# A state-space scan and an MLP on one core: units of one chunk of all four sequences instead of two chunks of one sequence, B and C transposed by VectorE

## The chip, the cores and the metric

One core of one Trainium2 chip. The time is the device time of one execution in microseconds (us), the median of the runs. Five engines work side by side, each through its own queue in order: TensorE (PE in the profile, its weight loads PEld), VectorE (DVE), ScalarE (ACT), GpSimd (POOL), and SyncE (SP), which only issues DMAs here. The tensors lie in the chip's main memory; what the engines read lies in SBUF (128 partitions); PE writes to PSUM (banks of 512 f32 per partition).

## What is computed

Four sequences of 768 steps, 8 heads, head size D = 32, state size N = 16. A scan with decay, chunk by chunk, and then an MLP over all 3,072 tokens (256 to 2,048 to 256, tanh-GELU):

```python
for c in range(nc):
    cum = np.cumsum(la, axis=-1)                        # la = log(clip(a, 1e-6, 1))
    L = np.exp(cum[:, :, :, None] - cum[:, :, None, :]) * causal
    M = np.einsum('bhin,bhjn->bhij', Cc, Bc) * L
    y_intra = np.einsum('bhij,bhjd->bhid', M, xc)
    y_inter = np.einsum('bhin,bhnd->bhid', Cc, state) * decay_to_i[:, :, :, None]
    y[:, :, sl] = y_intra + y_inter
    Bx = np.einsum('bhjn,bhjd->bhjnd', Bc, xc) * decay_from_j[:, :, :, None, None]
    state = decay_full[:, :, None, None] * state + np.sum(Bx, axis=2)
h = x @ w_in                                            # x: y as 3072 tokens x 256
g = 0.5 * h * (1.0 + np.tanh(c * (h + 0.044715 * h * h * h)))
out = g @ w_out
```

The kernels use chunks of 128 steps (the result doesn't depend on the chunk). The decay is put into B and C beforehand: with r the product of a from a step to the end of its chunk, B is multiplied by r and C by 1/r, so the causal product of the two needs only a 0/1 triangle.

## The kernel before

There are 24 chunks of 128 tokens, numbered sequence by sequence. A unit is one or two neighbouring chunks of one sequence (`UNITS`: chunk 0, chunk 1, then pairs; 13 units).

*Preparation per sequence.* `f_R` scans a on DVE into r, for all sequences at once; `f_RT` turns r with matmuls against an identity; `f_recip` takes 1/r. Then per sequence: `f_mul` multiplies B and C (DVE, 128x768), `f_T` turns them by six PE transposes each into PSUM, `f_E` copies them to SBUF (`bh`, `ch`), `f_F` makes `ce` (C with the odd and with the even heads set to zero, `par`), `f_N` turns B back by six more PE transposes and `f_bn` copies that out (`bn`). For the first sequence this is split (`sequence0`), and its first chunk has a short path of its own.

*State part per unit.* `f_G` makes the scores of two heads at a time in one of four row groups of PE (K = 32; partitions 32g to 32g+31 hold two heads), into four banks of PSUM, the tile `gb`. `f_M` multiplies a chunk's scores by the triangle (DVE, 128x1024, PSUM to bf16). `f_D` makes B times x, `f_S` adds it to the decayed state, `f_SP` spreads the state to a block-diagonal `sp_new` (both DVE). `f_Y` adds state and score terms in PSUM (`yb`), in four column groups of 32, and `f_yev` (ACT) evicts it as `xm`, the MLP's input. From unit 4 on, `f_YDG` issues Y of a unit with D and G of the next as one piece.

*MLP per unit.* `f_s1`: up-projection into one of two PSUM tiles `hp` (512 wide: four f-blocks of 128 tokens, or two of 256); `f_gelu` (ACT, 128x512); `f_s2`: down-projection of one chunk, 16 matmuls of 256 into `o_ps`; `f_oev` evicts, `f_store` stores 128 KB.

*Order.* All these are nodes with an engine, an assumed duration, dependencies and a priority. `run_order` plays them through before the kernel is built and fixes every engine's queue; PSUM tiles with one buffer (`gram` is `gb`, `yb`, `o`) are modelled as pools. On the chip each engine works its queue in that order and waits where data is missing. While the plan has PE idle and no down-projection has begun, `idle` puts filler matmuls on zeros (`wz`) in. SP's queue holds all loads but two, and the stores, in the plan's order; a DMA there waits for the one eight before it.

Of the kernel before, what the change touches and what calls it, by code (L numbers as in the profile page):

```python
# [8 lines left out]
FP32 = mybir.dt.float32  # L9
# [84 lines left out]
def kernel(  # L94
# [9 lines left out]
):  # L104
    nc = tc.nc

    batch, H, S, D = x.shape
    N = B.shape[-1]
    Q = 128
    CPB = S // Q  # L110
    R6 = CPB
    NCH = batch * CPB
    HC = CPB // 2
    HS = S // 2
    d_ff = moe_w_in.shape[1]
    d_model = moe_w_in.shape[0]
    n_tokens = batch * S
    NF = d_ff // 128
    UNITS = [[0], [1]] + [[c, c + 1] for c in range(2, NCH, 2)]
    NU = len(UNITS)  # L120

    const = ctx.enter_context(tc.tile_pool(name="const", bufs=1))
    ld = ctx.enter_context(tc.tile_pool(name="ld", bufs=batch))
    wfp = ctx.enter_context(tc.tile_pool(name="wfp", bufs=6))
    ldx = ctx.enter_context(tc.tile_pool(name="ldx", bufs=NU))
    xpool = ctx.enter_context(tc.tile_pool(name="xpool", bufs=6))
    work = ctx.enter_context(tc.tile_pool(name="work", bufs=2))
    msb = ctx.enter_context(tc.tile_pool(name="msb", bufs=4))
    st = ctx.enter_context(tc.tile_pool(name="st", bufs=4))
    GT_BUFS = 6  # L130
    gpool = ctx.enter_context(tc.tile_pool(name="gpool", bufs=GT_BUFS))
    opool = ctx.enter_context(tc.tile_pool(name="opool", bufs=6))
# [5 lines left out]


    a_t = const.tile([64, HS], FP32, name="a_t")  # L140
    a_half = [bass.AP(tensor=a.tensor, offset=a.offset + i * HS, ap=[[S, batch * H], [1, HS]])
              for i in range(2)]
    XF, X16 = {}, {}
    U = [dict() for _ in range(batch)]
    bc0 = const.tile([128, 2, H, N], FP32, name="bc0")

    def load_bc0(i, q):
        q.dma_start(out=bc0[:, i], in_=(B, C)[i][0, :, 0:Q, :].rearrange("h p n -> p h n"))

    def load_bc(b, i):  # L150
        d = U[b]
        if "bc" not in d:
            d["bc"] = ld.tile([128, 2, H, R6 * N], FP32, name="bc_t")
        nc.sync.dma_start(out=d["bc"][:, i],  # L154
                          in_=(B, C)[i][b].rearrange("h (p r) n -> p h (r n)", r=R6))

    nc.sync.dma_start(out=a_t[0:32], in_=a_half[0])
    nc.scalar.dma_start(out=a_t[32:64], in_=a_half[1])
    load_bc0(1, nc.sync)
    load_bc0(0, nc.scalar)  # L160

    wz = const.tile([128, 512], BF16, name="wz")
# [4 lines left out]
    ends = const.tile([64, Q], FP32, name="ends")  # L167
    nc.vector.memset(ends, 0.0)
    nc.vector.memset(ends[:, Q - 1:Q], 1.0)
    ac = const.tile([64, HS + 1], FP32, name="ac")  # L170
    nc.vector.memset(ac[:, HS:HS + 1], 0.0)
    pe1 = const.tile([64, HC], FP32, name="pe1")
    pe2 = const.tile([64, 2 * batch, HC], FP32, name="pe2")

    idf = const.tile([64, 64], FP32, name="idf")
    nc.gpsimd.memset(idf, 0.0)
    nc.gpsimd.affine_select(out=idf, in_=idf, pattern=[[-1, 64]], compare_op=ALU.not_equal,
                            fill=1.0, base=0, channel_multiplier=1)
    ident = const.tile([128, 128], BF16, name="ident")
    make_identity(nc, ident)  # L180
    bmask = const.tile([128, H * D], BF16, name="bmask")
    nc.gpsimd.memset(bmask, 1.0)
    bm3 = bmask.rearrange("p (h d) -> p h d", h=H)
    nc.gpsimd.affine_select(out=bm3, in_=bm3, pattern=[[-N, H], [0, D]],
                            compare_op=ALU.is_ge, fill=0.0, base=0, channel_multiplier=1)
    nc.gpsimd.affine_select(out=bm3, in_=bm3, pattern=[[N, H], [0, D]],
                            compare_op=ALU.is_ge, fill=0.0, base=N - 1, channel_multiplier=-1)
    tri = const.tile([128, Q], BF16, name="tri")
    make_upper_triangular(nc, tri, val=1.0, diag=True)
    tri_b = tri.rearrange("p (o q t) -> p o q t", o=1, q=1).to_broadcast([128, 4, 2, Q])  # L190

    sel8 = const.tile([64, H], FP32, name="sel8")
    nc.vector.tensor_reduce(out=sel8, in_=idf.rearrange("p (b h) -> p h b", h=H),
                            op=ALU.add, axis=mybir.AxisListType.X)
    selp = const.tile([64, H, N], FP32, name="selp")
    nc.vector.tensor_copy(out=selp, in_=sel8.rearrange("p (h o) -> p h o", o=1)
                          .to_broadcast([64, H, N]))
    m8 = const.tile([64, 2 * batch], FP32, name="m8")
    nc.gpsimd.memset(m8, 1.0)
    nc.gpsimd.affine_select(out=m8, in_=m8, pattern=[[-H, 2 * batch]], compare_op=ALU.is_ge,  # L200
                            fill=0.0, base=0, channel_multiplier=1)
    nc.gpsimd.affine_select(out=m8, in_=m8, pattern=[[H, 2 * batch]], compare_op=ALU.is_ge,
                            fill=0.0, base=H - 1, channel_multiplier=-1)
    par = const.tile([128, 2], FP32, name="par")
    bmp = bmask.rearrange("p (g e d) -> p e g d", g=4, e=2)
    for e in range(2):
        nc.vector.tensor_reduce(out=par[:, e:e + 1],
                                in_=bmp[:, e, :, 0:1].rearrange("p g o -> p (g o)"),
                                op=ALU.add, axis=mybir.AxisListType.X)
    r_t = const.tile([64, HS], FP32, name="r_t")  # L210

    rt = const.tile([128, R6, batch * H], FP32, name="rt")
    pt = const.tile([128, R6, batch * H], FP32, name="pt")
    q0 = const.tile([128, H], FP32, name="q0")
    bc0s = const.tile([128, 2, H, N], BF16, name="bc0s")
    ce0 = const.tile([128, 2, Q], BF16, name="ce0")
    bh0 = const.tile([128, Q], BF16, name="bh0")
    pend = const.tile([128, NCH], FP32, name="pend")
    WF = {}
    w_in_sb = const.tile([128, 2, d_ff], BF16, name="w_in_sb")  # L220
    w_out_sb = const.tile([128, NF, d_model], BF16, name="w_out_sb")
    xm = const.tile([128, 2, n_tokens], BF16, name="xm")


    gb = ps1.tile([128, 4, 512], FP32, name="gb")
    yb = ps1.tile([128, 512], FP32, name="yb")
    y4 = yb.rearrange("p (c w t) -> p c w t", c=2, w=2)
    rp0 = yb[:, 0:H]
    T6 = [gb[:, 2 * i, 0:S // 2].bitcast(BF16) for i in range(2)]
    T6_0 = [yb[:, 0:S // 2].bitcast(BF16), T6[1]]  # L230

    T0, DT, MT, RP = {}, {}, {}, {}
    state = {}
    gts, ops, hps, outs = {}, {}, {}, {}

    def load_x(u):
        b, c = divmod(UNITS[u][0], CPB)
        XF[u] = ldx.tile([128, 2, H, D], FP32, name="x_t")
        for k in range(len(UNITS[u])):
            nc.sync.dma_start(out=XF[u][:, k], in_=x[b, :, (c + k) * Q:(c + k + 1) * Q, :]  # L240
                              .rearrange("h p d -> p h d"))

    wi = moe_w_in.rearrange("(k d) f -> d k f", d=128)
    wo = moe_w_out.rearrange("(q p k) m -> q p k m", p=128, k=4)

    def load_wi(q):
        WF[("i", q)] = wfp.tile([128, 2, 512], FP32, name="wf")
        nc.sync.dma_start(out=WF[("i", q)], in_=wi[:, :, q * 512:(q + 1) * 512])  # L248

    def load_wo(q):  # L250
        WF[("o", q)] = wfp.tile([128, 4, d_model], FP32, name="wf")
        nc.sync.dma_start(out=WF[("o", q)], in_=wo[q])  # L252
# [9 lines left out]
    def f_wi(q, k0, k1, eng):  # L262
        for k in range(k0, k1):
            copy(eng, w_in_sb[:, k, q * 512:(q + 1) * 512].rearrange("d (k p) -> d k p", k=4),
                 WF[("i", q)][:, k].rearrange("d (p k) -> d k p", k=4))

    def f_wo(q, eng):
        copy(eng, w_out_sb[:, 4 * q:4 * q + 4], WF[("o", q)])


    def f_clip(i0, i1):
        nc.vector.tensor_scalar(out=ac[:, i0:i1], in0=a_t[:, i0:i1], scalar1=1e-6, scalar2=1.0,
                                op0=ALU.max, op1=ALU.min)

    def f_R(k):
        nc.vector.tensor_tensor_scan(out=r_t[:, k * Q:(k + 1) * Q][:, ::-1],
                                     data0=ac[:, k * Q + 1:(k + 1) * Q + 1][:, ::-1],
                                     data1=ends[:, ::-1], initial=1.0,
                                     op0=ALU.mult, op1=ALU.max)

    def f_RT0():
        nc.tensor.matmul(out=rp0, lhsT=r_t[0:32, 0:Q], rhs=idf[0:32, 0:H], start=True, stop=True,
                         skip_group_check=True)

    def f_RT(r0, r1):
        if r0 == 0:
            RP[1] = psh.tile([128, 512], FP32, name="hp")[:, 0:R6 * batch * H] \
                .rearrange("p (r j) -> p r j", r=R6)
# [524 lines left out]
```

## Time and profile before

| | |
|---|---|
| median of 3 runs | 124.88 us (124.67 to 126.23) |
| span of the profiled execution | 122.8 us |
| up-projection, 256 wide (L506) | 352 matmuls, and 64 of 128 wide |
| down-projection (L523) | 384 matmuls of 128x256 |
| gelu (L514, ACT) | 96 of 596 ns |
| first up-projection | starts at 11.95 us |
| first down-projection | starts at 22.2 us |
| last matmul | ends at 119.02 us |
| x loads | 24 of 128 KB, median 4.5 us from issue to landing (3.3 to 9.1) |
| B and C loads | 8 of 384 KB (4.4 and 5.4 us), 2 of 64 KB (2.8 and 4.2 us) |
| a | 2 of 48 KB (2.0 and 2.3 us) |

The span is that of one execution under the profiler, from its first to its last instruction; 2.1 us lie between it and the median. A group's line reads: line, engine, operation, output from input with shapes, count, then busy us and mean ns of one, then the idle time before them and what ended it. Matmuls overlap, so the pieces of the chain of waits, not the means of a group, tell what one costs in a row.

### The profile page before, as it was taken

The numbers are of one execution on the slowest core, as the hardware profiler recorded it, in microseconds if no ns is written. First come the engines' busy times: TensorE is split into PE (matmuls) and PEld (weight loads), VectorE is DVE, ScalarE is ACT, GpSimd is POOL, SyncE is SP. The second block draws the span as 40 slices with busy tenths as digits, with TensorE's granted clock in tenths as the row PEclk, the third lists the DMA queues.
The fourth block names the chain that finished last, engine by engine and source line by source line (L and its number), as shares of the span: only waits on it lengthen the run. The fifth ranks groups of instructions, "written<-read, shape, count | busy, mean of one in ns | idle before, by whom it ended". The sixth has DMA issues, their size and how long they took to land.

```text
span 122.8 us, 3507 instructions
## 1 busy us (share of the span) xinstructions
PE 114.6 (93%) x1506; PEld 96.2 (78%) x1506; DVE 68.3 (56%) x116; ACT 74.9 (61%) x145; POOL 23.0 (19%) x38
## 2 busy tenths in 40 slices
PE   5899978989799999999999999999999999999970
PEld 5687747778678798787879889787878888888860
DVE  3897999968849888184979672475663000000110
ACT  4025536674676677656686777865768766786310
POOL 7206967750320160122000000000000000000000
PEclk9975699999999999999999999999999999999999
DMA  3999959989799899851101101101110111100121
GB/s 52 242 266 265 328 112 370 320 191 200 128 229 221 127 235 216 145 134 48 43 0 48 43 0 48 43 0 48 43 43 5 45 43 45 45 21 22 43 90 43
DMA packets 40591, 14.09 MB, mean 115 GB/s; under 512 B 35904, under 2 KB 39040, under 8 KB 40576
## 3 DMA queue, kind: packets, MB, share of 16 engines
q1 hardware_dynamic: 39488, 13.75, 46.4%
q8 instruction: 12, 0.20, 0.7%
q10 hardware_dynamic: 1088, 0.11, 0.7%
q14 instruction: 3, 0.02, 0.1%
HBM read 10.72 MB, written 3.15 MB: 113 GB/s over the span
## 4 chain that ended last, share of the span: by engine, by line
PE 70%; SPq 18%; DMA 5%; DVE 3%; issue 1%; DVEq 0%
PE o_ps L523 29%; PE hp L506 29%; SPq L240 7%; DMA bc_t<-in_B_dram 5%; SPq L252 5%; SPq L154 4%; PE yb L523 3%; SPq L248 3%; PE gb L408 2%; PE yb L451 2%; PE yb L460 2%; PE gb L358 2%; DVE ch L260 2%; PE gb L379 1%; DVE bc L349 1%
## 5 line engine op out<-in xcount | busy, mean ns | idle before, releaser
L514 ACT ACTIVATE gT<-hp 128x512 bf16<-128x512 f32 x96 | 53.6, 596 | 24.4 <-PE hp L506 24.2
L506 PE MATMUL hp<-xm,w_in_sb 128*128 128x256 bf16 (+1 forms) x416 | 53.7, 267 | 0.9 <-POOL w_in_sb L258 0.4
L523 PE MATMUL o_ps<-w_out_sb,gT 128*128 128x256 bf16 x352 | 47.3, 273 | 0.0
L506 PEld LDWEIGHTS <-w_in_sb 128*128 128x128 bf16 x416 | 37.6, 99 | 7.7 <-issue 2.0
L523 PEld LDWEIGHTS <-gT 128*128 128x128 bf16 x384 | 37.1, 98 | 4.8 <-issue 0.4
L418 DVE TENSOR_TENSOR m<-gb,tri 128x1024 bf16<-128x1024 f32 (+1 forms) x25 | 29.1, 1173 | 1.9 <-PE gb L408 1.8
L532 DVE COPY o_sb<-o_ps 128x256 f32<-128x256 f32 x2 | 0.8, 424 | 25.6 <-PE o_ps L523 25.6
L258 POOL CAST x<-x_t 128x512 bf16<-128x512 f32 (+1 forms) x12 | 8.5, 710 | 25.0 <-DMA x_t<-in_x_dram 20.1
L479 DVE SCALAR_TENSOR_TENSOR s_new<-s_new,pend,hp 128x64 f32<-128x64 f32 x16 | 4.5, 279 | 11.5 <-PE hp L429 11.2
L776 PE MATMUL o_ps<-wz 128*128 128x128 bf16 x77 | 8.9, 267 | 1.3 <-DVE warm L165 1.3
L530 ACT ACTIVATE o_sb<-o_ps 128x256 f32<-128x256 f32 x20 | 7.7, 385 | 3.8 <-PE o_ps L523 2.1
L486 DVE SCALAR_TENSOR_TENSOR sp_new<-s_new,pend,bmask 128x256 bf16<-128x256 f32 x20 | 10.0, 506 | 0.0
L469 ACT ACTIVATE xm<-yb 128x512 bf16<-128x512 f32 (+1 forms) x13 | 7.3, 564 | 4.3 <-PE yb L460 2.1
L258 POOL CAST w_in_sb<-wf 128x512 bf16<-128x512 f32 x6 | 7.0, 1193 | 7.0 <-DMA wf<-in_moe_w_in_dram 7.0
L776 PEld LDWEIGHTS <-wz 128*128 128x128 bf16 x77 | 6.5, 122 | 1.8 <-DVE warm L165 1.2
L460 PE MATMUL yb<-m,x 128*32 128x128 bf16 x192 | 6.3, 223 | 0.6 <-DVE m L418 0.6
L373 DVE TENSOR_SCALAR ce<-ch,par 128x768 bf16<-128x768 bf16 (+2 forms) x10 | 5.9, 634 | 0.8 <-ACT ch L256 0.8
L451 PE MATMUL yb<-ce,sp_new 128*32 128x128 bf16 x160 | 5.3, 221 | 0.0
L408 PE MATMUL gb<-ce,bh 32*128 32x256 bf16 x96 | 5.1, 278 | 0.0
L460 PEld LDWEIGHTS <-x 128*32 128x32 bf16 x192 | 3.8, 97 | 1.5 <-issue 1.5
L358 PEld LDWEIGHTS <-bc 128*128 128x128 bf16 x48 | 3.8, 110 | 1.3 <-issue 1.1
L258 POOL CAST w_out_sb<-wf 128x1024 bf16<-128x1024 f32 x4 | 4.4, 1112 | 1.5 <-DMA wf<-in_moe_w_out_dram 1.5
(72 smaller groups left out, 61.6 us busy)
## 6 DMA issues: line engine op xcount, KB each, us to landing
x_t<-in_x_dram SPq DMA_DIRECT2D x24, 128.0 KB, 4.5
out_dram<-o_sb SPq DMA_DIRECT2D x24, 128.0 KB, 1.7
wf<-in_moe_w_in_dram SPq DMA_DIRECT2D x4, 512.0 KB, 6.9
wf<-in_moe_w_out_dram SPq DMA_DIRECT2D x4, 512.0 KB, 6.0
bc_t<-in_C_dram SPq DMA_DIRECT2D x4, 384.0 KB, 4.4
bc_t<-in_B_dram SPq DMA_DIRECT2D x4, 384.0 KB, 5.4
bc<-in_B_dram ACTq DMA_DIRECT2D x1, 64.0 KB, 4.2
bc<-in_C_dram SPq DMA_DIRECT2D x1, 64.0 KB, 2.8
```

Of the source, the lines that this page charges most:

```text
L240: nc.sync.dma_start(out=XF[u][:, k], in_=x[b, :, (c + k) * Q:(c + k + 1) * Q, :] .rearrange("h p d -> p h d"))
L258: nc.gpsimd.tensor_copy(out=o, in_=i)
L408: nc.tensor.matmul(out=gb[:, g, 256 * k:256 * k + 256], lhsT=bh_of(gc)[32 * g:32 * g + 32], rhs=ce_of(gc)[32 * g:32 * g + 32], start=True, ...
L418: nc.vector.tensor_tensor(out=MT[gc][:, g0:g1], in0=gb[:, g0:g1, 256 * k:256 * k + 256] .rearrange("p g (e t) -> p g e t", e=2), in1=tri_b ...
L451: nc.tensor.matmul(out=y4[32 * j:32 * j + 32, k, w], lhsT=sp[:, 32 * h:32 * h + 32], rhs=ce_of(gc)[:, h % 2], start=first(j), stop=False, ...
L460: nc.tensor.matmul(out=y4[32 * j:32 * j + 32, k, w], lhsT=X16[u][:, k, 32 * h:32 * h + 32], rhs=m[:, h // 2, h % 2, :], start=first(j), st ...
L486: nc.vector.scalar_tensor_tensor(out=sp_new.rearrange("p (g d) -> p g d", g=4), in0=state[("s", gc)].rearrange("p (o d) -> p o d", o=1).to ...
L506: nc.tensor.matmul(out=hp[:, j * nt:(j + 1) * nt], lhsT=w_in_sb[:, kc, fi * 128:(fi + 1) * 128], rhs=xm[:, kc, t0:t0 + nt], start=(kc == 0 ...
L514: nc.scalar.activation(gts[u][:, i * per:(i + 1) * per, 0:nt], hps.pop((u, i)).rearrange("p (j t) -> p j t", j=per), AF.Gelu_apprx_tanh)
L523: nc.tensor.matmul(out=ops[gc], lhsT=gts[u][:, fi, tt * Q:(tt + 1) * Q], rhs=w_out_sb[:, fi, :], start=(fi == 0), stop=(fi == NF - 1), ski ...
L530: nc.scalar.activation(o_sb, ops.pop(gc), AF.Copy)
L776: nc.tensor.matmul(out=zb[:, 0:128], lhsT=wz[:, 0:128], rhs=wz[:, 0:128], start=True, stop=True)
```

## The change

The whole body is rewritten around another unit: chunk c (0 to 5) of all four sequences, 512 tokens. Partitions 32b to 32b+31 now hold sequence b, with four steps in a partition's row, so a 32x32 block transposes in place on DVE, and row group b of PE works on sequence b.

- B and C come in 32-partition loads of 64 KB, one per chunk, sequence and tensor (48 instead of 10). `f_mul` and the transpose `f_T` are 128x512 per chunk, both DVE. The transposes of r are DVE's too; the reciprocal is one 128x128.
- `bn`, B with steps on partitions, is no longer a transpose: `f_bn` copies `bc16` from SBUF to SBUF, four DMAs of 32 KB per chunk, issued by SP after B's multiply.
- `f_S` keeps the state already decayed, 128x256; its spread form `spb` is written by POOL (`f_sp`, four copies of 32 partitions).
- Y, D and G are separate pieces; G and Y of a chunk come in two halves (w = 0, 1), each with two M.
- The up-projection of chunks 1 to 5 is 512 wide. Chunk 0 goes sequence by sequence, 128 wide.
- w_in is cast without a permutation; its columns are picked with a step of four when loaded as weights.
- The last down-projection, eviction and store are cut in two halves of 128 columns.
- Fillers, durations and priorities are set anew.

```diff
-    UNITS = [[0], [1]] + [[c, c + 1] for c in range(2, NCH, 2)]
+    NC = S // Q
+    R = 4
+    def load_bc(c, i, b, q):
+        t = get("bc", c, [128, 2, H, R * N], FP32)
+        q.dma_start(out=t[32 * b:32 * b + 32, i],
+                    in_=(B, C)[i][b, :, c * Q:(c + 1) * Q, :].rearrange("h (p r) n -> p h (r n)", r=R))
...
-    def f_T(b, i):
-        bc = U[b]["bc16"].rearrange("p i r h n -> p i r (h n)")
-        for r in range(R6):
-            nc.tensor.transpose(out=(T6 if b else T6_0)[i][:, r * 128:(r + 1) * 128], in_=bc[:, i, r], identity=ident)
+    def f_T(c, i):
+        nm = ("bT", "cT")[i]
+        t = get(nm, c, [128, G, Q], BF16)
+        nc.vector.transpose(out=t.rearrange("p g (q r) -> p g r q", r=R),
+                            in_=T[("bc16", c)][:, i].rearrange("p r (g k) -> p g r k", g=G))
...
+    def f_rT(i):
+        nc.vector.transpose(out=rT[i], in_=rr[i].rearrange("q (p r) -> q r p", r=R))
+    def f_qT(i):
+        nc.vector.reciprocal(qT[i], rT[i])
+    def f_bn(c, b):
+        t = get("bn", c, [128, NB, H * N], BF16)
+        nc.sync.dma_start(out=t[:, b], in_=T[("bc16", c)][32 * b:32 * b + 32, 0])
...
+    def f_G(c, w):
+        for g in (2 * w, 2 * w + 1):
+            for b in range(NB):
+                nc.tensor.matmul(out=gb[:, b, 256 * (g % 2):256 * (g % 2) + 256],
+                                 lhsT=T[("bT", c)][32 * b:32 * b + 32, g],
+                                 rhs=T[("ce", c)][32 * b:32 * b + 32, :, g, :],
+                                 start=True, stop=True, tile_position=(32 * b, 0))
+    def f_S(c):
+        d = T[("dt", c)][:, 0:H * D]
+        if c > 0:
+            s = P["st"].tile([128, H * D], FP32, name="st")
+            nc.vector.tensor_tensor(out=s, in0=T[("s", c)], in1=d, op=ALU.add)
+            d = s
+        t = P["st"].tile([128, H * D], FP32, name="st")
+        nc.vector.tensor_tensor(
+            out=t.rearrange("p (g k) -> p g k", g=G), in0=d.rearrange("p (g k) -> p g k", g=G),
+            in1=pend[:, c + 1].rearrange("p (g o) -> p g o", o=1).to_broadcast([128, G, 2 * D]),
+            op=ALU.mult)
+        T[("s", c + 1)] = t
+    def f_sp(c, b, eng):
+        ps = slice(32 * b, 32 * b + 32)
+        copy(eng, spb[c % 2][ps, b], T[("s", c)][ps])
+    def f_s1(c, f):
+        hp = psh.tile([128, 512], FP32, name="hp")
+        T[("hp", (c, f))] = hp
+        for kc in range(2):
+            nc.tensor.matmul(out=hp, lhsT=w_in5[:, kc, f // 4, f % 4], rhs=T[("xm", c)][:, kc],
+                             start=(kc == 0), stop=(kc == 1))
...
+        qn[i] = add("DVE", 0.22, f_qT, i, deps=[rn[i]], prio=p0 + 3)
...
-            def f_YDG(u):
-                f_Y(u)
-                f_D(u + 1)
-                f_G(u + 1)
-            Yn[u] = add("PE", 1.05, f_YDG, u, deps=deps, prio=q + 2)
+            for w in range(2):
+                g = Gn[(c, w)] = add("PE", 0.34, f_G, c, w, deps=[Tn[(c, 0)]] + Fn[c], prio=q + 2 + w)
+                ms = [add("DVE", 1.24, f_M, c, w, kk, deps=[g], prio=q + 2 + w + 0.1 * kk) for kk in range(2)]
+                Mn[(c, w)] = ms
+                g.takes("gA", ms[0]).takes("gB", ms[1])
+                y = Yn[(c, w)] = add("PE", 0.55, f_Y, c, w, deps=ms + xcn[c] + spn[c], prio=q + 4 + w)
```

## The prediction

> **What bounds the kernel now.** I read the page's busy shares and slices first, then the chain of waits, then the groups by shape, then the timeline of the first 40 us.
>
> ```profile
> PE 114.6 (93%) x1506; PEld 96.2 (78%) x1506; DVE 68.3 (56%) x116; ACT 74.9 (61%) x145; POOL 23.0 (19%) x38
> ...
> PEclk9975699999999999999999999999999999999999
> DMA  3999959989799899851101101101110111100121
> ```
>
> TensorE (PE) is full from the eleventh slice on, and nothing else is near full there. DMA is full from the second slice to the sixteenth (3 to 50 us). So there are two stages: one that waits for loads, one that is PE work end to end. The chain says where they meet:
>
> ```profile
> 24.08 5.77 DMA bc_t<-in_B_dram
> ...
> 29.87 0.96 DVE bc L349
> 30.82 0.88 DVE ch L260
> 31.74 0.49 PE gb L358 x6
> ...
> 35.19 0.44 PE o_ps L523 x4
> 35.63 0.33 PE gb L408 x8
> 35.96 0.54 PE o_ps L523 x4
> ...
> 94.32 0.23 PE yb L451 x8
> 94.55 0.11 PE yb L460 x8
> 94.66 0.11 PE yb L451 x8
> 94.77 0.11 PE yb L460 x8
> 94.88 0.98 PE hp L506 x8
> ...
> 119.10 0.42 DVE o_sb L532
> ```
>
> The columns are start, length, what. B of the second sequence lands at 29.9, and from 32 us the chain is PE pieces but for one wait of 0.97 us at 46. The MLP pieces cost 0.109 us per 128x256 matmul (0.87 for 8). An excursion into the state part costs more than itself: the first 8 matmuls of a Y take 0.23 against 0.11 for the next, and 8 MLP matmuls after it 0.98 against 0.87. So a Y with both neighbours is 0.23+0.33+0.11 = 0.67; a G alone 0.33+0.10 = 0.43 (the 4 matmuls behind it take 0.54, not 0.44); a D alone 0.17+0.10 = 0.27. Merged Y, D and G, as at 40.27, make 0.95.
>
> ```profile
> L418 DVE TENSOR_TENSOR m<-gb,tri 128x1024 bf16<-128x1024 f32 x23 | 27.8, 1217 | 1.9 <-PE gb L408 1.8
> L373 DVE TENSOR_SCALAR ce<-ch,par 128x768 bf16<-128x768 bf16 x6 | 2.6, 475 | 0.0
> L373 DVE TENSOR_SCALAR ce<-ch,par 128x384 bf16<-128x384 bf16 x2 | 2.2, 1144 | 0.0
> L305 DVE RECIPROCAL pt<-rt 128x144 f32<-128x144 f32 x1 | 1.0, 1039 | 0.0
> ```
>
> Busy us, then mean ns. The two 384-wide rows are the longer ones: they ran at 12.5 to 14.7 us, under POOL's weight casts (12.44 to 14.6).
>
> **What does not change.** The MLP: 768 matmuls' worth at 0.109 = 83.8 us; up-projections of chunks 1 to 5 become 512 wide, 160 instead of 320. 512-wide is not in the trace: between 0.213 (four times the 0.053 that a 128-wide one adds) and 0.218; I take 0.218, and 0.8 us is the most it can gain. Gelu, M, Y, G and D instructions keep number and shape.
>
> **The late stage, after minus before.** In before, 35.19 to 119.02 (83.8 us) holds the last 656 MLP matmuls of the 256 size (652 recorded) and the state part: pieces of 2.97 G, 4.70 Y, 2.18 transposes, 0.56 D, 0.97 wait, and 1.1 hidden in the neighbours' longer pieces: 12.5 in all. In the changed program's order, chunk 1's first up-projection (call its time T1) also has exactly 656 left: 16 of chunk 0's down-projection and five chunks of 128. Behind it stand eight G, eight Y, three D: 8 x 0.43 + 8 x 0.67 + 3 x 0.33 (sixteen matmuls each, 0.23+0.10) = 9.8, less 0.5 for five places where two of them are neighbours. So PE ends at T1 + 71.5 + 9.3 = T1 + 80.8. The removed PE transposes are worth 2.2 here, their wait 1.0; the unmerged excursions give a part back.
>
> **T1.** It stands behind Y of chunk 1, which wants x of chunk 1 from all four sequences. Time of the 16 DMA engines up to then, by the trace's packets (128 B 13.9 ns, 384 B 25.0, so 256 B some 19.4): an x load 64 packets per engine, 0.89 us; a B or C load now 16 packets, 0.31; weights 1.68 (w_in) and 1.41 (w_out) each. Changed order up to x of chunk 1: a 0.24, B and C of chunk 0 2.5, x 3.5, w_in 6.7, w_out 5.6, B and C of chunk 1 2.5, x 3.5, and eight new SBUF-to-SBUF loads for bn at 0.11 to 0.20: 25.8. The same sum of before up to B of sequence 1 is also 25.8, and that landed at 29.87. So x of chunk 1 lands near 30, 0.5 later if SP's queue starves a little, since the first bn copy waits on SP for DVE's second multiply and everything behind it (w_in 2 and 3, x, w_out) waits too. DVE gets there at: a landed 3.0, clip 0.2, scan 0.4, its transpose 0.25, reciprocal of 128x128 0.94 (1039 ns at 144 and 457 at 48), multiply 0.69, transpose 0.64, multiply 0.69: 7.3, since C's last load lands near 5.2. Some 5 us of loads are then in flight, so the cover is about there. DVE's 128x512 transpose is in no row: 0.32 (ce rate) to 3.1 (reciprocal rate); I take 0.64, the rate of the 128x768 PSUM copy (955 ns). At 3.1 the chain would grow by 2.5 per transpose and the cover be gone.
>
> Then POOL casts the last x (0.61): Y at 31.2. B and C of chunk 1 land at 21.6; multiplies, transposes and ce take 3.4 on DVE, G at 25, two M pairs 2.7 each: 30.5, in time. In PE's queue follow Y 0.67, D 0.33, pp 0.5, 4 MLP 0.44, Y 0.67, 12 MLP 1.31: T1 = 35.1.
>
> **Sum.** PE ends at 35.1 + 80.8 = 115.9. I add 0.5 for G of chunk 2, whose B transpose comes off DVE at 36.0 by the same rows, 0.4 after PE asks. Behind it 3.5 instead of 3.8 (122.8 - 119.02): the last eviction is half a tile, 0.28 (the 128x128 ACT row) for 0.42, and its store half as large. Span 119.9 against 122.8; the median of the runs is 2.1 over that span, so **122.0 us**. What is hidden and priced at nothing: POOL's four 32-partition state copies a chunk (0.11 to 0.43 each; Y is 4 us away; uncovered, 1.7 per chunk), ACT's ce and casts in the first 11 us (PE waits for loads), and the first chunk's x of sequence 2, landing at 16.4 by the same sums: ACT's eleven gelus behind it (0.6) end at 25, while G is awaited anyway.
>
> **Rivals.** *(E) Loads come earlier*: nothing starves, 512-wide is cheaper, no wait at chunk 2: T1 34.3 and 1 us off the rest, 120.1. For it: before's DMA has a dip to 0.31 at 16 to 18 us which the new order need not have.
>
> *(B) DVE held by POOL in chunk 1*: the multiplies and ce fall under w_out casts (1.04 to 1.33 each); with 0.7 for each of four, as the 1144 row has it, M ends at 33.5 and T1 is 36.5. PE would also idle 3 us, with no filler matmuls behind the first down-projection; before, an underfilled stretch was followed by half clock from 7.9 to 14.7. One 3.4 us stretch at half costs 1.7: 123.4 to 125.1, say 124.3.
>
> *(D) Small loads pay latency.* Eight DMAs are in flight at most in either order of waits on SP, and B and C now come as 64 KB. The 64 KB loads of before took 2.8 and 4.2 us to land; eight per 2.8 to 4.2 instead of 2.5, twice before T1, is 0.6 to 3.4 later: 124. The Trainium skill's page "DMA: Bandwidth & Descriptors", section "Rules for kernel authors", speaks against the change here: coalesce small transfers, since under 64 KB mostly overhead is paid. By that rule (D) would be the likeliest and the sum 124; by the rows the packets of a following DMA fill the engines meanwhile (DMA share 0.9 and over with 128 KB x loads).
>
> *(C) The ends swap: slower.* Both queues are fixed. G of each half chunk needs the M pair of the half before it, on the single score tile; M stands in DVE's queue behind the next chunk's multiplies, which wait for loads, and behind a reciprocal which the planner prices at 0.22 against 0.94. PE waits in order, with MLP matmuls queued behind. DVE has 9.1 us of work per chunk (4 M 4.9, two multiplies 1.4, two transposes 1.3, ce 0.7, state 0.8) against 16 of PE, which speaks against it; the 1.8 us for which M waited on G in the row above shows that the hand-over binds when it is late. There are eight such places after T1. Without the 0.5 counted above the sum is 121.5; at 0.42 us of PE wait each the gain is gone, over 0.74 it is slower by more than 2%, and at 1.0 it is 129.5.
>
> *(X) It does not do what it says*: the order shows no PE transpose left, so I give this nothing.
>
> **Chances and range.** Forecast 0.40, E 0.12, B 0.15, D 0.06, C 0.27. Within 2% means 122.4 to 127.4, about what a measurement of this kernel tells from no change. The forecast's own range is 120.8 to 123.4, three fifths of it under 122.4: 0.25 faster, 0.15 same. Faster 0.37, same 0.15 + 0.15 + 0.06 = 0.36, slower 0.27. The range runs from 119.6 (E) to 128.5, into C.
>
> **What would show it.** No PE rows with an identity; 160 512-wide matmuls at some 0.22; last x of chunk 1 cast at 30.6 to 31.5; first 512-wide matmul at 35.1; from there no PE wait over 0.5. Wrong would be: T1 over 37 (B, D), or waits of PE on M or ce of a microsecond in chunk after chunk (C).

## The result and the profile after

The changed kernel takes 142.15 us (median of 4 runs, 141.41 to 142.56), the kernel before 125.48 beside it (4 runs). The ratio is 1.133, 95% interval 1.124 to 1.142: slower. Where a kernel was timed several times, runs more than 1.5% above its fastest are slow ones and stay out of a comparison; here there are none. The profiled execution took 142.56, with a span of 140.9. The page of the changed kernel, busy time and slices:

```profile
PE 118.1 (84%) x1319; PEld 84.7 (60%) x1332; DVE 65.5 (47%) x91; ACT 72.3 (51%) x142; POOL 30.2 (21%) x66
...
PEclk9985557999996899999959999999999999999999
DMA  3897888936478458686484110101111111111121
```

DVE has less work than before (65.5 for 68.3), and DMA, full from 3 to 50 us before, is at 0.3 to 0.8 from the ninth slice to the twenty-second. PE is busy for 84% of the span instead of 93%, and its granted clock dips three times, not once. What PE waited for (in all, times, longest):

```profile
PE hp L402 <- DMA bn<-bc: 5.4, 5, 1.8
PE gb L363 <- DVE bT L310: 5.0, 4, 2.4
PE gb L332 <- DVE bT L310: 3.8, 1, 3.8
```

L402 is D, L363 is G of chunks 1 to 5, L332 the very first G. Between the first 512-wide matmul (T1) and the last matmul, PE's windows show busy time, matmuls recorded and granted clock:

```profile
40.04:137.54 97.50, 84.96 (x869) 0.96 0.33 74
```

T1 came at 40.04, predicted 35.1: 4.9 late. Then 97.5 us follow where 81.3 were predicted (80.8 + 0.5): 16.2 more. Of the 97.5, PE was idle 12.5, and two stretches of 3.4 us ran at half clock, which costs 3.4; the rest is 81.6, so the work itself was sized right to 0.8. Behind the last matmul 3.4 (3.5 predicted), outside the span 1.7 (2.1).

**Ahead of T1.** DVE's timeline of the changed kernel (start, length, what, and in brackets the idle time before it with what ended it):

```profile
19.86 0.29 DVE L280 TENSOR_SCALAR pe<-mR,ac,rr 128x16 f32<-128x16 f32 x1
24.52 0.42 DVE L416 TENSOR_TENSOR st<-hp,pend 128x256 f32<-128x256 f32 x1 [4.38 <-PE yb L350]
24.87 0.68 DVE L302 TENSOR_TENSOR bc<-bc,qT 128x512 bf16<-128x512 f32 x1
25.58 1.36 DVE L310 STREAM_TRANSPOSE cT<-bc 128x512 bf16<-128x512 bf16 x1
26.73 0.72 DVE L302 TENSOR_TENSOR bc<-bc,rT 128x512 bf16<-128x512 f32 x1
27.37 1.59 DVE L319 TENSOR_SCALAR ce<-cT,par 128x512 bf16<-128x512 bf16 x2
28.89 1.34 DVE L310 STREAM_TRANSPOSE bT<-bc 128x512 bf16<-128x512 bf16 x1
30.73 2.36 DVE L370 TENSOR_TENSOR m<-gb,tri 128x1024 bf16<-128x1024 f32 x2 [0.51 <-PE gb L363]
33.85 2.36 DVE L370 TENSOR_TENSOR m<-gb,tri 128x1024 bf16<-128x1024 f32 x2 [0.76 <-PE gb L363]
```

DVE stood 4.4 us for L416, S(0), the first state update, which needs D of chunk 0 (L402 on PE, at 24.09; the row names L350, which PE did right behind it). C of chunk 1, whose multiply is the 24.87 row, stood behind it in the queue. From there the chain runs through two transposes, ce, G and two M pairs to 36.1, with 0.5 and 0.8 us of waiting for G; T1 follows 3.9 later, as predicted.

SP waited with it: bn(1), the copies for chunk 1, need B's multiply and stood in its queue ahead of three x loads of chunk 1. So the last x was late too. SP's wait (in all, times, longest), POOL's cast of that x, and PE's rows:

```profile
SPq L324 <- DVE bc L302: 6.5, 2, 3.8
...
35.79 0.61 POOL L254 CAST x<-xf 128x512 bf16<-128x512 f32 x1 [2.58 <-DMA xf<-in_x_dram]
...
24.09 0.30 PE L402 MATMUL hp<-x,bn 128*32 128x64 bf16 x16
...
34.81 1.91 PE L456 MATMUL o_ps<-w_out_sb,gT 128*128 128x256 bf16 x16 [0.47 <-ACT ob L252]
36.65 0.41 PE L380 MATMUL yb<-ce,spb 128*32 128x128 bf16 x16
```

L380 opens Y of chunk 1, and PE did not wait for it: the work queued ahead of it ended just then. From 23 us to T1 PE waited 1.7 us in all. Three things thus end within 0.6 us: DVE's chain (36.1), the last x (36.4, predicted 31.2) and PE's own queue (36.65). Shortening one alone gains little.

**Behind T1** the same thing comes back in a loop. DVE again:

```profile
51.59 1.31 DVE L310 STREAM_TRANSPOSE cT<-bc 128x512 bf16<-128x512 bf16 x1
54.77 0.42 DVE L413 TENSOR_TENSOR st<-st,hp 128x256 f32<-128x256 f32 x1 [1.87 <-PE yb L380]
55.29 0.42 DVE L416 TENSOR_TENSOR st<-st,pend 128x256 f32<-128x256 f32 x1
55.63 0.61 DVE L319 TENSOR_SCALAR ce<-cT,par 128x512 bf16<-128x512 bf16 x2
56.16 0.68 DVE L302 TENSOR_TENSOR bc<-bc,rT 128x512 bf16<-128x512 f32 x1
56.88 1.32 DVE L310 STREAM_TRANSPOSE bT<-bc 128x512 bf16<-128x512 bf16 x1
```

The state update of chunk 2 (54.77) is late because D(2), right ahead of the L380 that its row names, waited on PE for bn until 54.43; the next chunk's ce, multiply and transpose of B stand behind it, and G of chunk 3 waits on PE until 58.25. Why bn was late is in SP's queue (issues of DMAs; a length covers the issue and what the queue stood for at it):

```profile
46.59 1.44 SPq L160 DMA_DIRECT2D bc<-in_B_dram  x3
48.13 0.55 SPq L324 DMA_DIRECT2D bn<-bc  x1
48.72 0.59 SPq L160 DMA_DIRECT2D bc<-in_B_dram  x1
49.35 0.45 SPq L165 DMA_DIRECT2D xf<-in_x_dram  x1
49.85 0.60 SPq L324 DMA_DIRECT2D bn<-bc  x1
```

Of the four copies of bn(2) two are here, though DVE had finished B's multiply at 42.1: loads stand between. Where the queue stood for nothing else, an issue took 0.45 to 0.6 us, for 32 KB as for 128 KB, and SP has 123 DMAs where it had 66 (the expectations below say 121 and 109 for 123 and 111).

### The profile page after: what moved, and what is told of

Same layout as the page of the kernel before. It is cut to its first block, busy times and chain, and to the rows that moved or that the text cites. A ratio compares the mean times of both kernels' runs of the same rounds, so it can differ in the third digit from the quotient of the medians.

```text
span 140.9 us, 3231 instructions
## 1 busy us (share of the span) xinstructions
PE 118.1 (84%) x1319; PEld 84.7 (60%) x1332; DVE 65.5 (47%) x91; ACT 72.3 (51%) x142; POOL 30.2 (21%) x66
## 4 chain that ended last, share of the span: by engine, by line
PE 53%; SPq 15%; DVE 12%; DMA 9%; issue 5%; ACT 2%; POOL 1%; DVEq 0%; POOLq 0%; ACTq 0%
PE o_ps L456 20%; PE hp L445 18%; SPq L160 8%; SPq L324 4%; DMA bc<-in_C_dram 4%; DVE bc L302 3%; PE hp L431 3%; DMA xf<-in_x_dram 3%; DVE bT L310 3%; PE yb L456 2%; SPq L165 2%; PE gb L332 2%; PE o_ps L678 2%; DMA bc<-in_B_dram 2%; DVE m L340 2%
## 5 line engine op out<-in xcount | busy, mean ns | idle before, releaser
L445 PE MATMUL hp<-xm,w_in_sb 128*128 128x512 bf16 x147 | 42.3, 392 | 1.2 <-ACT gT L450 0.7
L370 DVE TENSOR_TENSOR m<-gb,tri 128x1024 bf16<-128x1024 f32 x20 | 23.5, 1218 | 5.3 <-PE gb L363 5.2
L445 PEld LDWEIGHTS <-w_in_sb 128*128 128x128 bf16 x160 | 17.7, 116 | 10.8 <-issue 2.4
L254 POOL CAST x<-xf 128x512 bf16<-128x512 f32 (+1 forms) x12 | 7.0, 587 | 29.9 <-DMA xf<-in_x_dram 29.7
L254 POOL CAST spb<-st 32x256 bf16<-32x256 f32 x20 | 10.1, 505 | 13.6 <-DVE st L416 9.6
L252 ACT ACTIVATE ob<-o_ps 128x256 f32<-128x256 f32 x20 | 7.7, 386 | 7.6 <-PE o_ps L456 4.3
L431 PE MATMUL hp<-xm,w_in_sb 128*128 128x128 bf16 x128 | 11.3, 248 | 0.0
L396 ACT ACTIVATE xm<-yb 128x512 bf16<-128x512 f32 x10 | 6.0, 597 | 8.5 <-PE yb L388 8.5
L431 PEld LDWEIGHTS <-w_in_sb 128*128 128x128 bf16 x128 | 10.1, 124 | 0.4 <-issue 0.2
L363 PE MATMUL gb<-ce,bT 32*128 32x256 bf16 x80 | 4.4, 296 | 5.9 <-DVE bT L310 5.0
L310 DVE STREAM_TRANSPOSE cT<-bc 128x512 bf16<-128x512 bf16 x6 | 7.9, 1323 | 0.1
L310 DVE STREAM_TRANSPOSE bT<-bc 128x512 bf16<-128x512 bf16 x6 | 7.9, 1313 | 0.1
L402 PE MATMUL hp<-x,bn 128*32 128x64 bf16 x80 | 2.7, 196 | 5.5 <-DMA bn<-bc 5.4
L363 PEld LDWEIGHTS <-bT 32*128 32x128 bf16 x80 | 1.3, 93 | 9.2 <-DVE bT L310 6.4
L340 DVE TENSOR_TENSOR m<-gb,tri 128x1024 bf16<-128x1024 f32 x4 | 4.8, 1222 | 3.8 <-PE gb L332 3.8
```

The source lines that it names most:

```text
L252: nc.scalar.activation(o, i, AF.Copy)
L254: nc.gpsimd.tensor_copy(out=o, in_=i)
L310: nc.vector.transpose(out=t.rearrange("p g (q r) -> p g r q", r=R), in_=T[("bc16", c)][:, i].rearrange("p r (g k) -> p g r k", g=G))
L340: nc.vector.tensor_tensor(out=o.rearrange("p (k t) -> p k t", k=8), in0=gb[:, 2 * (b % 2):2 * (b % 2) + 2].rearrange("p k (j t) -> p (k j) ...
L370: nc.vector.tensor_tensor(out=t[:, 1024 * k:1024 * k + 1024].rearrange("p (k t) -> p k t", k=8), in0=gb[:, 2 * k:2 * k + 2].rearrange("p k ...
L431: nc.tensor.matmul(out=hp[:, j * Q:j * Q + Q], lhsT=w_in5[:, kc, i, j], rhs=T[("xm", 0)][:, kc, b * Q:b * Q + Q], start=(kc == 0), stop=(k ...
```

## The experiments

One time each beside the kernel before (124.65 to 125.96), except the last; the changed kernel's own runs spread by 1.2 us, and a reordered version, timed four times, by 3.3 over all four. So differences under some 3 us between reordered versions are not read as results. "Idle" is PE's idle time from T1 to the last matmul, "half" the time at a granted clock of 0.50, in all. T1 is not the same point of the work in every order: 48 down-projection matmuls are recorded ahead of it in the changed kernel, 44 in e4_plan, 24 in e5_s0late and z1_poolplan, 16 in e8_combo and p1_spplan.

| run | us | T1 | idle | half |
|---|---|---|---|---|
| changed kernel | 142.2 | 40.0 | 12.5 | 20.5 |
| e1_nobn | 135.0 | 39.1 | 8.2 | 13.7 |
| e2_bnpool | 135.7 | 40.1 | 8.0 | 17.1 |
| e3_fill | 142.5 | 39.4 | 12.9 | 17.1 |
| e4_plan | 136.5 | 38.1 | 8.5 | 17.1 |
| e5_s0late | 138.6 | 38.3 | 9.5 | 13.7 |
| e6_t2 | 155.5 | 48.4 | 14.9 | 41.0 |
| y_bnst | 135.8 | 39.6 | 8.5 | 17.1 |
| e8_combo | 129.6 | 37.3 | 2.1 | 10.2 |
| t_contig | 139.5 | 38.1 | 10.2 | 20.5 |
| z1_poolplan | 128.7 | 37.9 | 2.0 | 6.8 |
| d1_dummy | 141.3 | 39.0 | 10.4 | 20.5 |
| e7_x1 | 141.7 | 39.5 | 10.3 | 23.9 |
| p1_spplan | 136.1 | 36.7 | 7.0 | 13.7 |

The theories at the start: S, SP's single queue makes loads and bn late; V, DVE's transposes take twice what was predicted; K, the half clock from 9.3 to 23 us makes D(0) and all behind it late; P, the queues were planned with wrong durations.

**e1_nobn**

```diff
-        nc.sync.dma_start(out=t[:, b], in_=T[("bc16", c)][32 * b:32 * b + 32, 0])
+        pass
...
-                                 lhsT=T[("bn", c)][:, b, 32 * g:32 * g + 32],
+                                 lhsT=T[("x16", c)][:, b, 32 * g:32 * g + 32],
```

> The 20 copies of B into bn are left out; the state products read the x tile in place of bn, so B's part in the states is other data, while each engine but SP keeps its order and shapes. S (SP's queue): bn(1) no longer holds up the x loads of chunk 1 (issued at 29.75, 31.66, 32.3 in the changed kernel), so the first 512-wide matmul comes at 36 to 37 instead of 40.0; the waits of PE on bn after it (12 us in 14 places at most) go, PE idle behind it falls from 12.6 us to under 6, and the half-clock window near 71 us with it: 128 to 132 us. V (DVE transposes at 1.32 us): DVE's work is as it was, so the time stays over 138. K (half clock from 9.3 to 23): the first 512-wide matmul moves by under 1 us and the time by as much. P (the plan's durations): 135 to 139, since the fixed orders of the other engines stay.

135.0 us: the waits on bn go, the waits on bT stay (6.6 us). But T1 moved by 0.9 only, though the last x of chunk 1 was cast by 32.1 (36.4 in the changed kernel). S is right about where the time behind T1 goes, but 135.0 is not its 128 to 132 (idle 8.2 us, not under 6), and it is wrong about T1: that came 15.9 us after D(0), as in the changed kernel, with x 4.3 earlier.

**e2_bnpool**

```diff
-        nc.sync.dma_start(out=t[:, b], in_=T[("bc16", c)][32 * b:32 * b + 32, 0])
+        nc.gpsimd.dma_start(out=t[:, b], in_=T[("bc16", c)][32 * b:32 * b + 32, 0])
```

> The 20 bn copies are issued by POOL instead of SP, in the same places of the plan. S: SP has 101 DMAs left and nothing in its queue waits for DVE before a load, so loads come earlier: first 512-wide matmul at 36 to 38, PE idle after it 6 to 9 instead of 12.6, 132 to 137 us; the casts of x on POOL then stand behind bn's wait, which can give some of it back. V and K: no change, 140 to 143. P: no change beyond 2 us.

135.7: all of it behind T1, which stayed at 40.09. S again for the later part, within its range; not for T1.

**e3_fill**

```diff
+        m = n + (60 if n == 53 else 0)
         def fill():
-            for _ in range(n):
+            for _ in range(m):
```

> 60 more of the small warm-up matmuls on PE ahead of the first G, 113 for 53, so that PE does not idle from 6.5 to 10.4 us. K: the half clock of 9.3 to 23 us does not come or is a window of 3.4 us; D of chunk 0 comes 1.5 to 3 us earlier, with it the multiply behind S(0) on DVE, bn and x of chunk 1: first 512-wide matmul at 37 to 38, 138 to 140 us. S and V: the clock may change, the first 512-wide matmul stays within 1 us of 40.0 and the time within 1.5 of 142, since SP and DVE set it.

The first half-clock stretch began near 14 instead of 9.4 and was half as long, D(0) came 1.3 earlier, T1 0.7 earlier; the time did not move, with three stretches of half clock behind T1 instead of two. So K ahead of T1 is not by itself the cause of the time. T1 came 15.9 to 16.5 us after D(0) in the changed kernel and these three runs.

**e4_plan** changes only the numbers given to the planner, such as

```diff
-            Tn[(c, i)] = add("DVE", 0.6, f_T, c, i, deps=[muln[(c, i)]], prio=q + 1.1 - 0.6 * i)
+            Tn[(c, i)] = add("DVE", 1.2, f_T, c, i, deps=[muln[(c, i)]], prio=q + 1.1 - 0.6 * i)
```

> The planner gets the durations that the trace shows (a 3.0, 64 KB loads 0.5, transposes of 128x512 1.2, reciprocal 0.93, multiply 0.7, rT 0.40, ce 0.4 and 0.7, bn 0.58, state copies 0.5) and puts the same instructions into another order on each engine. P: the waits of PE on bT, ce and bn after the first 512-wide matmul fall from 12.6 us to under 6, 132 to 136 us. S: SP's 121 issues stay, so do the late loads: 138 to 143. V: DVE's work stays and T1 within 1 us of 40: 139 to 142.

136.5, against S's 138 to 143 and in P's direction: waits on bT fell from 5.0 to 1.5, those on bn rose to 6.3. T1 is 2 earlier. The order counts: the work is the same but for fillers (118 recorded instead of 112).

S(0) on DVE had now taken the place of x as the suspected reason for T1. **e5_s0late**

```diff
     cst2.deps.append(Mn[(0, 3)])
+    Sn[0].deps.append(Tn[(1, 0)])
```

> The first state update S(0) stands on DVE behind the two multiplies, transposes and ce of chunk 1 instead of ahead of them. The runs before this one showed x of chunk 1 is not what the first 512-wide matmul waits for (it came at 40.09 with bn on POOL and at 39.14 with no bn at all); theory O (DVE's order) takes its place: DVE stood idle from 20.1 to 24.5 us for S(0), with the multiply of C of chunk 1, whose load was there, behind it. O: that multiply at 21 to 22.5 instead of 24.87, G of chunk 1 at 27 instead of 30.2, M ends at 33 instead of 36.1 and the first 512-wide matmul at 37 instead of 40.0; the time falls by 2 to 3.5 us, to 138.5 to 140. S (SP's queue sets it): bn(1) issued earlier too, but the first 512-wide matmul within 1 us of 40. V: the transposes still take 1.15 each behind one another, no change from their side.

138.6. DVE's timeline of this run:

```profile
21.90 0.69 DVE L302 TENSOR_TENSOR bc<-bc,qT 128x512 bf16<-128x512 f32 x1 [1.44 <-DMA bc<-in_C_dram]
...
26.98 0.44 DVE L416 TENSOR_TENSOR st<-hp,pend 128x256 f32<-128x256 f32 x1
...
30.53 2.35 DVE L370 TENSOR_TENSOR m<-gb,tri 128x1024 bf16<-128x1024 f32 x2 [0.50 <-PE gb L363]
```

The multiply came at 21.9, when its load landed (21.6 in the prediction), and M ended at 32.9, 3.2 earlier. O holds for the chain. T1 gained only 1.8 of it, with 24 down-projection matmuls (2.6 us) fewer ahead of it in this order, since the next things were close: the last x, cast at 33.75, then the a-chain of chunks 4 and 5, for which PE waited 1.3 us at 36.1 (L280). The rest of the 3.5 us came behind T1: 3.0 us less idle time, and one stretch of half clock instead of two.

**e6_t2**

```diff
         nc.vector.transpose(out=t.rearrange("p g (q r) -> p g r q", r=R),
                             in_=T[("bc16", c)][:, i].rearrange("p r (g k) -> p g r k", g=G))
+        nc.vector.transpose(out=t.rearrange("p g (q r) -> p g r q", r=R),
+                            in_=T[("bc16", c)][:, i].rearrange("p r (g k) -> p g r k", g=G))
```

> Each of the twelve 128x512 transposes on DVE is made twice, into the same tile, nothing else changed: 12 x 1.15 to 1.3 us = 14 to 16 us more on DVE, in the same order. V and O: the chain DVE-G-M in front of the first 512-wide matmul holds two transposes of chunk 1, so it moves from 40.0 by 2.3 for these and up to 2.3 for those of chunk 0 in front of the first G: 42.5 to 44.5. After it, V (DVE is late in every chunk): most of the eight later transposes comes through, 150 us or more in all. S: after it only the transposes of chunks 2 and 3 are waited for, since DVE has 16 us a chunk: 145 to 148.

155.5, 13.3 more for 12 transposes of 1.15 to 1.3: V's 150 or more holds, S's 145 to 148 does not. The place is not V's: T1 moved by 8.4, more than the 4.6 that the chain ahead of it holds, while the half clock doubled to 41 us; behind T1 4.6 came through, half of what the other eight transposes add. DVE's length costs ahead of T1 above all.

**t_contig**

```diff
-        nc.vector.transpose(out=t.rearrange("p g (q r) -> p g r q", r=R),
+        nc.vector.transpose(out=t.rearrange("p g (r q) -> p g r q", r=R),
```

> DVE's 128x512 transposes write their tile in one piece instead of every fourth element; the 128 steps of a chunk then stand in another order within B's and C's transposes, so the scores belong to other step pairs, with the same shapes and number of instructions. If the strided write is what made them 1.32 us where 0.64 was predicted: 0.6 to 0.7 each, and, as the doubled transposes cost 13.3 us for 14 to 16 more on DVE, 5 to 7 us off the changed kernel's 142. If the transpose takes its time whatever the write: 1.3 each and 141 to 143.

The groups of the changed kernel, then of this run (busy us, then mean ns of one):

```profile
L310 DVE STREAM_TRANSPOSE cT<-bc 128x512 bf16<-128x512 bf16 x6 | 7.9, 1323 | 0.1
L310 DVE STREAM_TRANSPOSE bT<-bc 128x512 bf16<-128x512 bf16 x6 | 7.9, 1313 | 0.1
```

```profile
L310 DVE STREAM_TRANSPOSE cT<-bc 128x512 bf16<-128x512 bf16 x6 | 4.2, 705 | 0.1
L310 DVE STREAM_TRANSPOSE bT<-bc 128x512 bf16<-128x512 bf16 x6 | 4.2, 702 | 0.1
```

So the strided write nearly doubles the transpose's time. But 139.5, not 135 to 137: T1 2.0 earlier, 1.1 gained behind it, together less than 3 us. V is a part of T1 at most.

**y_bnst** (on e2_bnpool)

```diff
-        nc.sync.dma_start(out=out[b * S + c * Q:b * S + c * Q + Q, :], in_=T[("ob", (c, b))])
+        nc.gpsimd.dma_start(out=out[b * S + c * Q:b * S + c * Q + Q, :], in_=T[("ob", (c, b))])
```

> bn copies and the full stores of the output are issued by POOL; SP keeps loads only. S: against bn on POOL alone (135.7 us) the waits of stores on evictions no longer hold loads back, PE's idle time after the first 512-wide matmul falls further, 132 to 135. Against S: POOL's casts of x now stand behind stores that wait for evictions: 135.7 or more.

135.8: no gain over bn alone. Either the stores on SP do not bind, or POOL's casts, now behind them, gave the gain back; the run does not tell.

**e8_combo** joins e2_bnpool, e4_plan and e5_s0late.

> Three edits at once: bn on POOL, the plan made with the measured durations, S(0) behind chunk 1's multiplies and transposes on DVE. If the three causes are separate, the gains add: 6.7 (bn) + 6 (plan) + 2.5 (S(0)) less what the first two share; the plan's gain lay mostly in waits on bT, bn's in waits on bn and loads, so 128 to 131 us. If plan and bn cure the same waits: 133 to 135. First 512-wide matmul at 36 to 37.5.

129.6. PE from T1 to the last matmul:

```profile
37.28:124.24 86.96, 84.91 (x904) 1.00 0.35 80
```

Idle 2.1 us of 87 and full clock: the stage behind T1 is PE work end to end, as the prediction had it (with 35 recorded matmuls more behind T1 than in the changed kernel).

**z1_poolplan** (on e8_combo)

```diff
-                n = add("SP", 0.58, f_bn, c, b, deps=[muln[(c, 0)]], prio=q, done=2.2)
+                n = add("POOL", 0.6, f_bn, c, b, deps=[muln[(c, 0)]], prio=q, done=2.2)
```

On it, **z2_fill** adds 35 warm-up matmuls as e3_fill did 60, **z3_x1** has the x loads of e7_x1 below, **z5_contig** the transposes of t_contig.

> As the run with three edits at once (129.6), but the planner counts bn as POOL's work, 0.6 each, so that POOL's casts of w_out and x are placed around it: in that run PE waited 2.6 us for a cast of w_out at 22.9, with POOL standing at a bn copy. If that wait is what is left: 126.5 to 128.5. If the load order sets T1: 129 to 130.

> z1_poolplan with 35 more of the small warm-up matmuls ahead of the first G, so that PE does not idle there. K (half clock): one or two of the half-clock windows of 3.41 us between 9 and 31 us go, 1 to 3 us less than z1_poolplan. If PE waits for DVE and loads in that stretch anyway: within 0.7 of it.

> z1_poolplan with the x of chunks 2 to 5 as one load of 512 KB each instead of four of 128 KB: 12 fewer issues on SP. S (SP's issues are what is left): the waits of PE after the first 512-wide matmul fall by 1 us or more, and the time by 1 to 2. If SP no longer binds: within 0.7 of z1_poolplan, or later by up to 1 since the casts wait for the whole load.

> z1_poolplan (128.7) with the transposes written in one piece, 0.70 us each for 1.32; the 128 steps of a chunk stand in another order in B's and C's transposes, so the scores belong to other step pairs. V: what is left against the prediction is the price of the transposes on the chain to the first 512-wide matmul (four, 0.6 each), 126 to 127. If loads and the half clock set that chain: 128 to 129.

128.7, with PE's wait for a cast of w_out down only from 2.6 to 2.0 us; then 131.4, 130.0 and 129.8. None is apart from z1 by more than its own spread, so what each of the three edits is worth on the best order stays open. z5_contig was idle for 0.1 us behind T1; its T1 came at 40.5, behind a 3.7 us wait for a cast of w_out and 17 us of half clock.

It was left to tell SP's number of DMAs from bn's place in its queue. **d1_dummy** (on e2_bnpool)

```diff
+        nc.sync.dma_start(out=dm[:, NB * c + b], in_=wz[:, 0:128])
```

> bn copies on POOL as in the run that gave 135.7, and in their old places on SP 20 copies of 32 KB of zeros into an unused tile, which wait for nothing: SP has its 121 DMAs again, but none that waits for DVE's multiply. If S is the number of issues: 20 x 0.55 us = 11 us more on SP, 140 to 143 us, like the changed kernel. If S is the wait in the queue, with loads behind it: 135 to 137.

**e7_x1**

```diff
+        nc.sync.dma_start(out=t.rearrange("p b h d -> p (b h) d"),
+                          in_=x[:, :, c * Q:(c + 1) * Q, :].rearrange("b h p d -> p (b h) d"))
...
-        load_x_n(c, 0, 1, 2, 3)
+        xl[(c, 0)] = load(3.5, load_x4, c)
+        for b in range(1, NB):
+            xl[(c, b)] = xl[(c, 0)]
```

> The changed kernel with the x of chunks 2 to 5 as one load of 512 KB each instead of four of 128 KB: SP has 109 DMAs instead of 121 and the same bytes; bn stays on SP with its wait for DVE. S by number: 12 x 0.55 = 6.6 us less on SP after the first 512-wide matmul, which stays at 40 (no x of chunk 1 is merged): 136 to 139. S by bn's wait: within 1.5 us of 142, since the bn copies stand where they stood. V: no change.

**p1_spplan**: e8_combo with bn back on SP.

> The plan with measured durations and S(0) behind chunk 1's work on DVE, with the bn copies still on SP: against the same with bn on POOL (129.6) it has the wait in SP's queue alone. If that wait costs by itself: 133 to 136, with the waits of PE on bn back at 4 us or more. If the better order has cured it: 129 to 131.

d1_dummy, 141.3: the copies that wait for no one bring back 5.6 of the 6.4 us, so the number counts. e7_x1, 141.7: 12 issues fewer, with bn still in the queue, gain nothing, where by number alone 12 of 20 would be worth 3.4. That speaks for the place as well but does not show it, for a chunk's x now lands as a whole, and half clock grew by 3.4 us. What PE waited for in d1_dummy, then in e7_x1:

```profile
PE gb L366 <- DVE bT L312: 4.1, 4, 2.0
PE yb L383 <- POOL spb L256: 2.3, 4, 1.3
PE gb L366 <- DVE m L373: 2.2, 1, 2.2
```

```profile
PE gb L368 <- DVE bT L310: 5.3, 4, 2.5
PE hp L407 <- DMA bn<-bc: 4.5, 5, 1.6
```

The first waits for what comes of late loads (the multiply of C at 55.25 waited 2.0 for its load, with an M pair behind it), the second still for bn. How the 6.4 us divide between number and place stays open; taking bn off SP's queue with nothing in its place gained them. And 136.1 for p1_spplan: with the better order, bn on SP still costs 6.4 against e8_combo, with 5.1 us of waits on bn.

**z1_rounds**

> The same kernel as z1_poolplan (one time of 128.7 beside 125.0), timed in three rounds beside the kernel before: 128 to 130 us, a ratio of 1.02 to 1.04 to before. If the single time was an outlier: a ratio whose interval holds 1.00.

129.2 us against 124.9 over the runs that count (two and five): 1.03. All four times lie between 128.4 and 131.7. No version here beats the kernel before.

## Why the prediction was wrong

- *T1 = 35.1* failed in its DVE term: "multiplies, transposes and ce take 3.4 on DVE, G at 25, two M pairs 2.7 each: 30.5, in time". The start was 24.87 instead of 21.6, behind S(0): 3.3 (with S(0) later, in e5_s0late, it was 21.90). The 3.4 became 5.4: 0.5 and 0.7 more for the transposes, 0.8 for ce under POOL's casts. The M pairs took 5.9 for 5.4. So DVE ended at 36.1 and not 30.5. The x term failed by as much, 36.4 for 31.2: the step saw SP wait for the first bn copy, at 0.5, and not for bn(1), where SP stood 3.8. But x did not set T1: cast by 32.1 in e1_nobn, it left T1 15.9 us behind D(0). Left out altogether was PE's own queue, busy from D(0) to T1 but for 1.7 us, with 13.6 us at half clock ahead of D(0). What would have set T1 with only one of the three cured was not taken apart. The landing at 21.6 was right (21.9 in e5_s0late).
- *The transpose at 0.64* was mis-sized, at 1.32 with its strided write; 0.70 in one piece.
- *Half clock*, 20.5 us for 6.8 before. The prediction saw one stretch of it in rival B. It went with PE's idle time here: with 2.1 us of it or less behind T1 (e8_combo, z1_poolplan) no stretch came there, with 7.0 or more one to five did.
- *"From there no PE wait over 0.5"* is the large failure: 12.0 of the 16.2, and 3.4 of half clock with it. The step priced bn "at 0.11 to 0.20" of DMA engine time and named SP's wait only for the first copy. It left out that each of 57 added DMAs holds SP for some 0.5 us, and that bn sits behind loads and loads behind bn. e2_bnpool takes away 4.5 of the idle time, e8_combo 10.4.
- *Rival C* had the form right, fixed queues with late work standing in front of ready work, and a price (129.5) for eight hand-overs of G and M; M was waited for once behind T1 (0.7 us). The item in front was S, the releasers bn and bT.
- *Rival D* had the cause of late loads right in part, but put it down to the latency of small loads, and priced it only ahead of T1. The 64 KB loads landed 2.5 to 2.8 us after their issue (medians on SP), no slower than before; it was their issues that came late. The Trainium skill's page "DMA: Bandwidth & Descriptors", section "Rules for kernel authors", says that spreading DMAs over several issuing engines gains no bandwidth and saves only issue time. Here that issue time was a part of what bound: the same copies from POOL give 135.7 for 142.2, while the DMA engines were at a share of 0.33 from T1 on.
- *The late PE sum*, 80.8, was right: 81.6 without waits and half clock, and e8_combo and z1_poolplan have a stage that is PE from end to end.

What is left in z1_rounds: PE ends at 124.6, not at the 116.4 of the sum. Of these 8.2 us, about 1.7 is idle time behind T1, 3.6 is T1 itself, and 2.6 are 24 down-projection matmuls that stand behind T1 there instead of ahead of it. So some 6 us lie ahead of T1. That they come from casts of w_out, half clock and loads is read from the traces and was not taken apart by a run.

## What to carry to other kernels

Count the DMAs of each issuing queue, not only the bytes: 123 issues at half a microsecond are some 60 us of a queue that also has to be in time for every stage. Where queues are fixed ahead, find for each wait what stands behind it on its engine; an update that nobody needs for 10 us can hold the multiply that the next stage begins with. Before shortening the chain that seems to set a time, see what else ends within a microsecond of it: here DVE's chain, x and PE's own queue did. A planner fed with wrong durations turns a small pricing error into a wrong order: the right numbers and two moves were worth 12.5 us of 142 with no work removed.

## What the runs showed of the hardware

- DVE's transpose of 128x512 bf16 takes 0.70 us written in one piece and 1.32 when written to every fourth element. The Trainium skill's page "Advanced Engine Details and Errata", section "VectorE Performance Modes", ties the double rate at 16 bits to unit steps; the two rows agree with that, though its table of instructions does not list the transpose.
- An issue took SP 0.45 to 0.6 us, for 32 KB as for 128 KB, and POOL 0.54 for 32 KB (2.16 for 4, z1_poolplan).
- Half clock (granted 0.50) came in stretches of 3.4 us or multiples of it, after PE had been underfilled (in the changed kernel idle from 6.5 to 10.4 and from 41.7 to 44.0, and busy for 0.7 of the 4 us from 66 to 70; the stretches begin at 9.4, 43.5 and 70.8); 60 more matmuls ahead of the first moved it to 13.9 and halved it, without gain.
